# Pooled attention and an MLP mixer in one kernel: the first batch's row maxima as the bias of the exponential, loads of q and k changed about, and a new order of the first steps

## The chip, the cores and the metric

The kernel runs on one core of a Trainium2 chip. The metric is the device time of one execution in microseconds, the median of several runs.

## What is computed

Eight batches, eight heads, 576 rows, 64 columns a head. Keys and values are averaged over groups of 8 rows, so each head has 72 pooled keys. The softmax of q times the pooled keys weighs the pooled values. Then a mixer over tokens (576 to 256 to 576) and one over channels (512 to 1536 to 512), each with a residual.

```python
k_p = k.reshape(B, H, Sp, pool, D).mean(axis=3)      # Sp = 72, pool = 8
v_p = v.reshape(B, H, Sp, pool, D).mean(axis=3)
scores = scale * np.matmul(q, k_p.transpose(0, 1, 3, 2))   # scale = 1/8
scores = scores - np.max(scores, axis=-1, keepdims=True)
attn = np.exp(scores)
attn = attn / (np.sum(attn, axis=-1, keepdims=True) + 1e-09)
x = np.matmul(attn, v_p)                             # heads side by side: B, 576, 512
h = np.maximum(xt @ w_tok1, 0.0) @ w_tok2            # xt = x, tokens last
u = x + h.transpose(0, 2, 1)
out = u + np.maximum(u @ w_ch1, 0.0) @ w_ch2
```

## The kernel before

**Rows.** Of a batch's 576 rows the first 512 are laid out four to a partition (row 4p + j); the last 64, the tail, share a 128-partition tile with another batch's tail. A batch's attention is three units: `a` (j = 0, 1), `c` (j = 2, 3) and the tail `t`. In the code `a, c, t` are batch 0's, `a1, c1, t1` batch 1's, and so on.

**One unit's steps.** `qT` turns q by matrix transposes and `copy_qT` copies it out of PSUM. `S(i)` makes the scores of one PSUM bank: bank 0 holds heads 0 to 2, bank 1 heads 3 to 5, bank 2 heads 6 and 7, each with two rows j and 72 columns (432, 432 and 288 columns). `shift(i)` is VectorE's: a maximum over each 72 columns (line 396) and a subtraction that writes `sh` to SBUF (line 398). `do_E(i)` is ScalarE's Exp of a whole bank with the scale 1/8 (line 406), into `prob_m`. `PT` turns the probabilities on TensorE, `copy_PT` copies them out (line 421 on either engine, line 544 for the tail), `AV` multiplies with the pooled values (lines 443, 445), `norm` divides (lines 451, 452). Pooled keys come from `pool_half` and `copy_half` for batch 0 (lines 308 to 320), from `sum_k` and `copy_k` for batch 1, both by matmuls with `pool_m`; pooled values from `pool_v` and `copy_v` (line 349). `prob_m` and `prob_t` are padded from 72 to 128 columns for the transposes that a DMA does in later batches; `clear_probs` zeroes that padding (all of `prob_t`).

**Token and channel mix.** `A_step` and `A` multiply with w_tok1 (line 635), `act_A` is a relu, `u` multiplies with w_tok2 (line 651, and line 649 for an identity), `turn_u` and `copy_uT` turn the result. The channel mix makes `GT` (lines 1007 and 1039) and then the output tiles in three parts each (line 1023), part 2 with the last third of w_ch2. w_tok2 is loaded as `w2r`, and GpSimd copies it into `w2m` (`split_w_tok2`, line 245), which line 651 reads.

**Order.** All loads with a change of type (fp32 to bf16) are issued by GpSimd in one queue, in the order of the calls at the end of the function (`load`, `load_w_tok`, `load_w_ch1`, ...). Half of batch 0's k comes by SyncE as fp32 and is converted by VectorE (line 210). The compute engines follow an order written out by hand: `begin()` lists the first steps, one call a line, and each engine runs its own in that order. The first list (batch 0's attention and token mix, to `weave(Stream(), st)`) is issued as it stands. The second (batch 1's attention and token mix) is woven into batch 0's channel mix by `weave`, which compares the running sums of the given costs. `fill`, `warm` and the numbers behind `S` and `AV` are idle matmuls on a zero tile (line 261) that keep TensorE busy. PSUM has six buffers `pa` and two `pt`, each given on in the order in which they come free.

Of the kernel before, what the change touches and what calls it, by code (L numbers as in the profile page):

```python
# [48 lines left out]
def kernel(  # L49
# [67 lines left out]
    def load(b, which=(0, 1, 2)):  # L117
        g = group_of[b]
        if (b == 2 or g > 1 and slot_of[b] == 0) and b not in main_t:
            tail_t[b] = [tail_pool.tile([P, H, D], BF16, name=n) for n in ("kt", "qt")]  # L120
            if b == 2:
                for t in tail_t[b]:
                    nc.gpsimd.memset(t[half[0]], 0.0)
            else:
                tail_t[groups[g][1]] = tail_t[b]
        main_t.setdefault(b, [None] * 3)
        for i in which:
            src = (k, q, v)[i]
            if i == 2 and b > 1:

                main_t[b][i] = v_pool.tile([P, H, POOL, D], BF16, name="vs")
                if b != 3:
                    load_v(b)
                continue
            mt = (v_pool.tile([P, H, POOL, D], BF16, name="vs")[:, :, 0:NJ, :] if i == 2 else
                  kv_pool.tile([P, H, NJ, D], BF16, name=("km", "qm")[i]))
            main_t[b][i], tt = mt, tail_t[b][i]
            nc.gpsimd.dma_start(out=mt.rearrange("p h j d -> p h (j d)"),
                                in_=src[b, :, 0:MAIN, :].rearrange("h (p j) d -> p h (j d)", j=NJ))

            for bb in [b] if g < 2 else groups[g] if slot_of[b] == 0 else []:
                nc.gpsimd.dma_start(out=tt[half[slot_of[bb]]], in_=src[bb, :, MAIN:S, :].rearrange("h p d -> p h d"))
# [30 lines left out]
    nc.vector.memset(pool_m, 1.0 / POOL)  # L173
# [7 lines left out]
    nc.vector.memset(diag, 1.0 / POOL)  # L181
# [31 lines left out]
    prob_m = [singles.tile([P, 2, H, P], BF16, name=f"prob_m{i}") for i in range(NPB)]  # L213
    prob_t = [singles.tile([P, 2, HP, P], BF16, name=f"prob_t{i}") for i in range(2)]
# [133 lines left out]
    def copy_v(b):  # L348
        nc.scalar.activation(out=vpx[b % NB][:, :, 0:D], in_=vp_of[b], func=AF.Copy, scale=float(POOL))
# [11 lines left out]
    class Unit:  # L361
# [31 lines left out]
        def shift(self, i):  # L393
            sc, n = self.sc[i], (BANKS[i][1] - BANKS[i][0]) * 2
            mx = sm_pool.tile([P, 8], FP32, name="mx")
            nc.vector.tensor_reduce(out=mx[:, 0:n], in_=sc, axis=AX.X, op=ALU.max)  # L396
            sh = sh_pool.tile([P, 6, SP], FP32, name="sh")
            nc.vector.tensor_tensor(out=sh[:, 0:n], in0=sc, in1=mx[:, 0:n, None].broadcast_to([P, n, SP]),  # L398
                                    op=ALU.subtract)
            self.sh[i] = sh  # L400

        def do_E(self, i):
            h0, h1 = BANKS[i]
            if self.probs is None:
                self.probs = prob_m[(2 * self.b + self.jj) % NPB]
            nc.scalar.activation(out=self.probs[:, :, h0:h1, 0:SP].rearrange("p e h n -> p h e n"),  # L406
                                 in_=self.sh[i][:, 0:(h1 - h0) * 2].rearrange("p (h e) n -> p h e n", e=2),
                                 func=AF.Exp, scale=scale)
# [68 lines left out]
    class TailUnit:  # L477
# [49 lines left out]
        def do_E(self):  # L527
            self.probs = prob_t[self.g % 2]
            for i, sh in enumerate(self.sh):
                nc.scalar.activation(out=self.probs[:, i, :, 0:SP], in_=sh[:, 0:HP], func=AF.Exp, scale=scale)  # L530
# [223 lines left out]
    def begin():  # L754
# [6 lines left out]
        add(0, fill, 17)  # L761
        add(0, fill, 9)
        add(0, c.qT, 0, HP)
        add(0, pool_half, 0)
        add(0, pool_half, 1)
        add(0, c.copy_qT, 0, HP, nc.scalar.copy)
        add(0, copy_half, 0, 1, nc.scalar.copy)
        add(0, copy_half, 0, 0, nc.vector.tensor_copy)
        add(0, a.qT, 0, HP)
        add(0, c.S, 0, 1)  # L770
        add(0, copy_half, 1, 0, nc.vector.tensor_copy)
        add(0, a.copy_qT, 0, HP, nc.scalar.copy)
        add(0, a.S, 0, 1)
        add(0, c.qT, HP, H)
        add(0, a.qT, HP, H)
        add(0, copy_half, 1, 1, nc.scalar.copy)
        add(0, a.copy_qT, HP, H, nc.scalar.copy)
        add(0, a.S, 2)
        add(0, warm, 9)
        add(0, a.S, 1)  # L780
        add(0, a.shift, 0)
        add(0, t.turn_q)
        add(0, c.copy_qT, HP, H, nc.scalar.copy)
        add(0, c.S, 1)
        add(0, a.shift, 2)
        add(0, c.shift, 0)
        add(0, a.do_E, 0)
        add(0, a.shift, 1)
        add(0, c.S, 2)
        add(0, a.do_E, 2)  # L790
        add(0, pool_v, 0)
        add(0, t.copy_qT)
        add(0, a.do_E, 1)
        add(0, c.do_E, 0)
        add(0, a.PT, 0)
        add(0, c.shift, 2)
        add(0, c.shift, 1)
        add(0, c.do_E, 2)
        add(0, a.copy_PT, 0, nc.vector.tensor_copy)
        add(0, t.S)  # L800
        add(0, a.PT, 1)
        add(0, t.shift)
        add(0, copy_v, 0)
        add(0, a.AV, 0, 1)
        add(0, c.do_E, 1)
        add(0, a.copy_PT, 1, nc.scalar.copy)
        add(0, t.do_E)
        add(0, a.norm, 0)
        add(0, c.PT, 0)
        add(0, a.AV, 1, 1)  # L810
        add(0, c.copy_PT, 0, nc.scalar.copy)
# [3 lines left out]
        add(0, t.PT)  # L815
        add(0, c.copy_PT, 1, nc.scalar.copy)
        add(0, c.norm, 0)
        add(0, c.AV, 1)
        add(0, t.copy_PT, nc.scalar.copy)
        add(0, c.norm, 1)  # L820
        add(0, t.AV)
        add(0, t.norm)
        add(0, m0.A_step, (0,))
        add(0, m0.A_step, (1,))
        add(0, m0.A_step, (2,))
        add(0, m0.A_step, (3,))
        add(0, m0.A_step, (4,))
        add(0, m0.act_A, 0)
        add(0, a1.qT)
        add(0, m0.act_A, 1)  # L830
        add(0, m0.u, 2)
        add(1800, a1.copy_qT, 0, H, nc.vector.tensor_copy)
        add(0, m0.u, 1)
        add(0, m0.add_u, 2)
        add(0, m0.u, 0)
        add(0, m0.add_u, 1)
        add(0, m0.add_u, 0)
        add(0, m0.u, 3)
        add(0, m0.turn_u, 1)
        add(0, m0.turn_u, 0)  # L840
        add(0, m0.add_u, 3)
        add(0, sum_k, 1)
        add(0, m0.turn_u, 2)
        add(0, m0.copy_uT, 1, nc.vector.tensor_copy)
        add(1170, copy_k, 1, 1)
        add(0, m0.copy_uT, 0, nc.scalar.copy)
        add(0, m0.copy_uT, 2, nc.vector.tensor_copy)
        add(0, m0.turn_u, 3)
        add(0, copy_k, 1, 0)
        add(0, m0.copy_uT, 3, nc.vector.tensor_copy)  # L850
# [4 lines left out]
        add(0, a1.S, 1)  # L855
        add(0, c1.qT)
        add(0, t1.turn_q)
        add(0, a1.S, 0)
        add(0, a1.S, 2)
        add(1170, c1.copy_qT, 0, H, nc.scalar.copy)  # L860
        add(0, load, 3, (2,))
        add(0, c1.S, 0)
        add(1060, a1.shift, 1)
        add(1060, a1.shift, 0)
        add(0, c1.S, 1)
        add(0, a1.do_E, 1)
        add(0, load_v, 3, 0, 2)
        add(848, a1.shift, 2)
        add(0, a1.do_E, 2)
        add(1800, t1.copy_qT)  # L870
        add(0, a1.do_E, 0)
        add(1378, c1.shift, 0)
        add(1060, c1.shift, 1)
        add(0, pool_v, 1)
        add(0, c1.S, 2)
        add(0, a1.PT, 0)
        add(0, sum_v, 2)
        add(212, c1.shift, 2)
        add(0, c1.do_E, 0)
        add(216, copy_v, 1)  # L880
        add(0, c1.do_E, 1)
        add(0, c1.do_E, 2)
        add(0, a1.PT, 1)
        add(0, t1.S)
        add(1060, t1.shift)
        add(350, a1.copy_PT, 1, nc.scalar.copy)
        add(0, pair_k, 3)
        add(1400, a1.copy_PT, 0, nc.vector.tensor_copy)
        add(1150, a1.do_AV, 0)
        add(0, t1.do_E)  # L890
        add(0, c1.PT, 0)
        add(1400, c1.copy_PT, 0, nc.vector.tensor_copy)
        add(0, c1.PT, 1)
        add(140, c1.copy_PT, 1, nc.scalar.copy)
        add(0, t1.PT)
        add(910, t1.copy_PT, nc.vector.tensor_copy)
        add(1495, c1.do_AV, 0)
        add(0, c2.qT)
        add(1495, t1.do_AV)
        add(1150, c1.do_AV, 1)  # L900
        add(920, a1.do_AV, 1)
        add(0, sum_k, 2)
        add(1170, c2.copy_qT)
        add(0, m1.A, 0)
        add(180, copy_k, 2, 1)
        add(864, m1.act_A, 0)
# [3 lines left out]
        add(0, a2.qT)  # L910
        add(0, m1.u, 2)
        add(0, copy_k, 2, 0)
        add(138, m1.add_u, 1)
        add(0, m1.u, 3)
        add(690, m1.add_u, 3)
        add(0, m1.u, 0)
        add(552, m1.add_u, 2)
        add(720, a2.copy_qT)
        add(0, sum_v, 3, 0, 2)
        add(138, m1.add_u, 0)  # L920
        add(0, m1.uT, 2, 2)
        add(0, m1.uT, 0, 2)
        add(0, t2.turn_q)
        add(900, t2.copy_qT)
# [158 lines left out]
    load(2, (1, 0, 2))  # L1083
# [43 lines left out]
```

## Time and profile before

| | us |
|---|---|
| median of 3 runs | 280.03 (279.56 to 281.25) |
| the profiled execution | 279.91 |
| its span, first to last instruction | 277.8 |
| TensorE busy | 267.6 (96%) |
| VectorE, ScalarE, GpSimd busy | 166.0, 121.8, 113.3 |
| granted TensorE clock | 1.0 throughout |

In the lines of the profile PE is TensorE and PEld its weight loads, DVE VectorE, ACT ScalarE, POOL GpSimd, SP SyncE; a q behind the name is the engine's sequencer. L398 is line 398 of the kernel. In the timeline a row gives the start and the duration in us, the engine, the line, the operation, what it writes and reads, the shape, how many were merged, and in brackets how long the engine was idle before it and who ended that. The view of the loads gives the median time from issue to landing of the loads issued in a stretch.

### The profile page before, as it was taken

How to read it: one execution, taken by the hardware profiler on the slowest of the kernel's cores; microseconds unless marked ns; L12 is line 12 of the kernel's file. 1: busy time of each engine (PE TensorE's matmuls, PEld its weight loads, DVE VectorE, ACT ScalarE, POOL GpSimd, SP SyncE). 2: the span in 40 equal slices, each digit the busy share in tenths (PEclk: the TensorE clock that was granted, in tenths of full speed). 3: DMA queues.
4: the chain of work that ended last, by engine and by line, in shares of the span. 5: the costliest groups of instructions: out<-in, count | busy, mean ns of one | idle time of the engine just before them, and what ended most of it. 6: DMA issues, size and time to landing. Idle time of an engine off the chain costs nothing.

```text
span 277.8 us, 5476 instructions
## 1 busy us (share of the span) xinstructions
PE 267.6 (96%) x2144; PEld 145.2 (52%) x2172; DVE 166.0 (60%) x383; ACT 121.8 (44%) x225; POOL 113.3 (41%) x160
## 2 busy tenths in 40 slices
PE   6789999999999999999999999999999999999994
PEld 4465856554545454474545454475545454554463
DVE  6597677778759852694479762775479452520112
ACT  8673688235533463045534452054623550036220
POOL 8758434696539857185349263930000000000000
PEclk9999999999999999999999999999999999999999
DMA  8999999996999999979997999858376700461013
GB/s 140 185 195 206 199 205 196 190 206 135 200 151 190 213 245 155 227 158 175 166 184 149 191 200 189 177 138 143 82 78 154 186 4 38 113 97 38 38 40 113
DMA packets 98969, 42.27 MB, mean 152 GB/s; under 512 B 68800, under 2 KB 94400, under 8 KB 98944
## 3 DMA queue, kind: packets, MB, share of 16 engines
q0 software_dynamic: 35616, 17.93, 49.6%
q1 hardware_dynamic: 63184, 23.93, 42.1%
q8 instruction: 17, 0.28, 0.4%
q10 hardware_dynamic: 144, 0.07, 0.1%
q14 instruction: 8, 0.07, 0.1%
HBM read 35.85 MB, written 9.44 MB: 163 GB/s over the span
## 4 chain that ended last, share of the span: by engine, by line
PE 89%; DVE 4%; DMA 2%; ACT 1%; issue 1%; POOL 1%; DVEq 0%; POOLq 0%
PE pa L1023 33%; PE pa L1007 31%; PE pa L672 3%; PE pa L390 3%; PE pa L468 3%; DMA km<-in_k_dram 2%; PE pa L597 2%; PE pa L651 1%; PE pa L615 1%; DVE xm L473 1%; PE pt L615 1%; PE pa L1039 1%; PE pt L374 1%; PE pa L677 1%; PE pa L635 1%
## 5 line engine op out<-in xcount | busy, mean ns | idle before, releaser
L1023 PE MATMUL pa<-wc,GT 128*128 128x512 bf16 (+2 forms) x426 | 102.5, 373 | 1.0 <-issue 0.2
L1009 ACT ACTIVATE GT<-pa 128x512 bf16<-128x512 f32 x105 | 62.1, 597 | 61.7 <-PE pa L1007 61.5
L1007 PE MATMUL pa<-uTm,wc 128*128 128x512 bf16 x372 | 89.1, 379 | 0.0
L1007 PEld LDWEIGHTS <-wc 128*128 128x128 bf16 x564 | 45.0, 98 | 36.7 <-issue 1.0
L1023 PEld LDWEIGHTS <-GT 128*128 128x128 bf16 x444 | 40.8, 98 | 41.5 <-issue 1.2
L406 ACT ACTIVATE prob_m<-sh 128x432 bf16<-128x432 f32 (+1 forms) x48 | 24.5, 522 | 55.2 <-DVE sh L398 55.1
L1027 DVE TENSOR_TENSOR o<-pa,um 128x512 f32<-128x512 f32 (+2 forms) x33 | 22.1, 670 | 28.6 <-PE pa L1023 28.5
L357 POOL TENSOR_TENSOR s<-vs 72x512 f32<-72x512 bf16 x24 | 27.6, 1150 | 14.8 <-DMA vs<-in_v_dram 13.4
L398 DVE TENSOR_TENSOR sh<-pa,mx 128x432 f32<-128x432 f32 (+1 forms) x48 | 26.8, 558 | 4.1
L396 DVE TENSOR_REDUCE mx<-pa 128x6 f32<-128x432 f32 (+1 forms) x48 | 26.4, 550 | 4.5 <-PE pa L390 4.3
L473 DVE TENSOR_TENSOR xm<-pa,den 128x256 bf16<-128x256 f32 x56 | 23.7, 424 | 1.9
L472 DVE RECIPROCAL den<-pa 128x4 f32<-128x4 f32 x60 | 10.5, 176 | 17.7 <-PE pa L468 17.5
L1055 POOL DMA_DIRECT2D out_dram<-o x1 | 0.6, 622 | 48.6 <-DVE o L1027 48.6
L673 DVE TENSOR_TENSOR um<-pa,xm 128x512 bf16<-128x512 f32 x24 | 16.1, 688 | 5.6 <-PE pa L672 4.3
L358 POOL TENSOR_TENSOR s<-s 72x256 f32<-72x256 f32 x24 | 17.3, 721 | 1.9
L390 PE MATMUL pa<-kbd,qT 128*128 128x144 bf16 x128 | 15.2, 226 | 0.9 <-ACT qT L378 0.7
L390 PEld LDWEIGHTS <-qT 128*128 128x128 bf16 x128 | 10.6, 98 | 9.3 <-ACT qT L378 1.3
L468 PEld LDWEIGHTS <-pT 72*128 72x128 bf16 (+1 forms) x256 | 11.4, 100 | 7.1 <-issue 0.8
L672 PE MATMUL pa<-AT,w2m 128*128 128x512 bf16 x45 | 13.1, 379 | 0.0
L468 PE MATMUL pa<-vpx,pT 72*128 72x65 bf16 (+1 forms) x256 | 12.6, 194 | 0.0
L269 POOL COPY kk<-km 128x1024 bf16<-128x1024 bf16 x8 | 8.1, 1037 | 10.8 <-DMA km<-in_k_dram 10.8
L1007 PE MATMUL pa<-uTt,wc 128*128 128x128 bf16 x192 | 11.9, 219 | 0.0
(151 smaller groups left out, 269.1 us busy)
## 6 DMA issues: line engine op xcount, KB each, us to landing
out_dram<-o SPq DMA_DIRECT2D x30, 256.0 KB, 2.6
vs<-in_v_dram POOLq DMA_DIRECT2D x7, 512.0 KB, 11.1
km<-in_k_dram POOLq DMA_DIRECT2D x7, 512.0 KB, 9.5
qm<-in_q_dram POOLq DMA_DIRECT2D x7, 512.0 KB, 12.7
wc<-in_moe_w_ch_dram POOLq DMA_DIRECT2D x6, 512.0 KB, 11.8
out_dram<-o SPq DMA_DIRECT2D x8, 128.0 KB, 2.4
o<-in_k_dram SPq DMA_DIRECT2D x2, 256.0 KB, 2.9
kt<-in_k_dram POOLq DMA_DIRECT2D x8, 64.0 KB, 7.8
```

The costliest lines, as they stand in the source:

```text
L357: nc.gpsimd.tensor_tensor(out=s4, in0=vs[:, hs, 0:4], in1=vs[:, hs, 4:8], op=add)
L390: nc.tensor.matmul(out=sc[:, (h - h0) * 2:(h - h0) * 2 + 2, :], lhsT=qTs[self.b][:, 2 * h + self.jj, :], rhs=kbd[self.b % NB][:, h], start ...
L396: nc.vector.tensor_reduce(out=mx[:, 0:n], in_=sc, axis=AX.X, op=ALU.max)
L398: nc.vector.tensor_tensor(out=sh[:, 0:n], in0=sc, in1=mx[:, 0:n, None].broadcast_to([P, n, SP]), op=ALU.subtract)
L406: nc.scalar.activation(out=self.probs[:, :, h0:h1, 0:SP].rearrange("p e h n -> p h e n"), in_=self.sh[i][:, 0:(h1 - h0) * 2].rearrange("p ...
L468: nc.tensor.matmul(out=ao[r, hh, :], lhsT=probs_of(h, r), rhs=vpx[b % NB][:, h, :], start=True, stop=True)
L473: nc.vector.tensor_tensor(out=xo[rows, hf * HP * D:(hf + 1) * HP * D].rearrange("p (h d) -> p h d", d=D), in0=ao[rows, :, 0:D], in1=den[ro ...
L672: nc.tensor.matmul(out=u_ps, lhsT=w2m[:, m, j, :], rhs=ATs[b][:, m, :], start=(m == 0), stop=(m == 1))
L1007: nc.tensor.matmul(out=g_ps[:, i, :], lhsT=wc1[:, kk, m * P:(m + 1) * P], rhs=uTs(kk, 0, width), start=(kk == 0), stop=(kk == 3))
L1009: nc.scalar.activation(out=GT[:, m0:m0 + per, :], in_=g_ps, func=AF.Relu)
L1023: nc.tensor.matmul(out=hold["ps"], lhsT=GT[:, kk, j * P:(j + 1) * P], rhs=wc2[:, kk, cols], start=(kk == 0), stop=(kk == NM - 1))
L1027: nc.vector.tensor_tensor(out=o_sb, in0=hold["ps"], in1=us(j)[:, cols], op=ALU.add)
```

## The change

- **Scale.** The 1/8 of the softmax moves into the pooling matrices (`pool_m`, `diag`), Exp loses its scale, and `copy_v` multiplies by pool/scale. (1/8 is exact in bf16.)
- **Maximum as bias.** `shift(i, True)` makes the negated maximum alone and leaves the scores in PSUM; `do_E` then runs one Exp for each head and row j, 72 columns, with that maximum as its bias. Three banks of batch 0 do so: `c` bank 0, `a` banks 0 and 1. The others stay as they were.
- **Loads.** q's first half goes ahead of k's tail. w_tok goes ahead of batch 1's k and q; the last third of w_ch1 ahead of `split_w_tok2`; the last third of w_ch2 behind batch 2.
- **Clears.** `prob_m` and `prob_t` become one tile, and one GpSimd memset of its padding stands behind the first third of w_ch1. Two memsets for batch 2's tails go from GpSimd to VectorE.
- **Order.** Both lists of `begin()` are rewritten: some copies change between ScalarE and VectorE, idle matmuls are placed anew, one token-mix step stands ahead of the tail's values, and the weave puts batch 1's `m1.A` ahead of the third part of the first output tile.

```diff
+    load_main0(q, main_t[0][1], 0, HP)
     load_tail0(k, tail_t[0][0])
-    load_main0(q, main_t[0][1], 0, HP)
...
-    nc.vector.memset(pool_m, 1.0 / POOL)
+    nc.vector.memset(pool_m, scale / POOL)
...
-    prob_m = [singles.tile([P, 2, H, P], BF16, name=f"prob_m{i}") for i in range(NPB)]
-    prob_t = [singles.tile([P, 2, HP, P], BF16, name=f"prob_t{i}") for i in range(2)]
+    prob_all = singles.tile([P, NPB + 1, 2, H, P], BF16, name="probs")
+    prob_m = [prob_all[:, i] for i in range(NPB)]
+    prob_t = [prob_all[:, NPB, i].rearrange("p (e h) n -> p e h n", e=2) for i in range(2)]
...
-        for t in prob_m:
-            nc.any.memset(t.rearrange("p e h n -> p (e h) n")[:, :, SP:P], 0.0)
-        for t in prob_t:
-            nc.any.memset(t, 0.0)
+        nc.gpsimd.memset(prob_all.rearrange("p t e h n -> p (t e h) n")[:, :, SP:P], 0.0)
...
-        def shift(self, i):
+        def shift(self, i, biased=False):
             sc, n = self.sc[i], (BANKS[i][1] - BANKS[i][0]) * 2
             mx = sm_pool.tile([P, 8], FP32, name="mx")
+            if biased:
+                nc.vector.tensor_reduce(out=mx[:, 0:n], in_=sc, axis=AX.X, op=ALU.max, negate=True)
+                self.sh[i] = (sc, mx)
+                return
...
+            if isinstance(self.sh[i], tuple):
+                sc, low = self.sh[i]
+                for h in range(h0, h1):
+                    for e in range(2):
+                        o = 2 * (h - h0) + e
+                        nc.scalar.activation(out=self.probs[:, e, h, 0:SP], in_=sc[:, o, :], func=AF.Exp,
+                                             bias=low[:, o:o + 1])
+                return
...
+        add(0, fill, 11)
+        add(0, fill, 16)
+        add(0, pool_half, 0)
         add(0, c.qT, 0, HP)
         add(0, pool_half, 1)
+        add(0, a.qT, 0, HP)
+        add(0, c.qT, HP, H)
         add(0, c.copy_qT, 0, HP, nc.scalar.copy)
+        add(0, a.qT, HP, H)
+        add(0, a.copy_qT, 0, HP, nc.vector.tensor_copy)
         add(0, c.S, 0, 1)
+        add(0, a.S, 0)
+        add(0, c.shift, 0, True)
+        add(0, a.shift, 0, True)
...
+        add(0, c.AV, 1, 1)
         add(0, t.copy_PT, nc.scalar.copy)
+        add(0, m0.A_step, (0,))
+        add(0, t.AV)
...
+    load_w_tok()
     load(1, (0, 1))
-    load_w_tok()
     load_w_ch1(0)
+    clear_probs()
     load_w_ch1(1)
     load_w_ch2(0)
     load(1, (2,))
+    load_w_ch1(2)
     split_w_tok2()
-    load_w_ch1(2)
     load_w_ch2(1)
+    load(2, (1, 0, 2))
     load_w_ch2(2)
-    clear_probs()
-    load(2, (1, 0, 2))
     load(3, (1, 0))
```

More of the change, by code (lines that the diff above doesn't have):

```diff
@@ L122, in load @@
                 for t in tail_t[b]:
-                    nc.gpsimd.memset(t[half[0]], 0.0)
+                    nc.vector.memset(t[half[0]], 0.0)
             else:
@@ L348, in copy_v @@
     def copy_v(b):
-        nc.scalar.activation(out=vpx[b % NB][:, :, 0:D], in_=vp_of[b], func=AF.Copy, scale=float(POOL))
+        nc.scalar.activation(out=vpx[b % NB][:, :, 0:D], in_=vp_of[b], func=AF.Copy, scale=POOL / scale)
     def sum_v(b, h1=0, h2=H):
@@ L889, in begin @@
[L889 to L891 removed]
+        add(0, load, 3, (2,))
+        add(848, a1.shift, 0)
+        add(0, a1.S, 1)
+        add(1170, c1.copy_qT, 0, H, nc.vector.tensor_copy)
+        add(0, c1.S, 0)
+        add(0, a1.S, 2)
+        add(530, a1.shift, 1)
+        add(0, a1.do_E, 1)
+        add(212, a1.shift, 2)
+        add(1060, c1.shift, 0)
+        add(0, c1.S, 1)
+        add(1378, c1.shift, 1)
+        add(0, a1.do_E, 0)
+        add(0, c1.S, 2)
@@ new lines, in begin @@
+        add(0, a1.do_E, 2)
+        add(0, pool_v, 1)
+        add(0, a1.PT, 0)
+        add(0, c1.do_E, 0)
+        add(212, c1.shift, 2)
+        add(1800, t1.copy_qT)
+        add(0, c1.do_E, 1)
+        add(0, t1.S)
+        add(910, a1.copy_PT, 0, nc.vector.tensor_copy)
+        add(0, c1.do_E, 2)
+        add(0, load_v, 3, 0, 2)
+        add(0, sum_v, 2)
+        add(1060, t1.shift)
+        add(540, copy_v, 1)
+        add(0, c1.PT, 0)
+        add(0, t1.do_E)
+        add(0, a1.PT, 1)
+        add(560, a1.copy_PT, 1, nc.scalar.copy)
```

161 lines of the change are left out of this document (62 added, 99 removed).

## Prediction

> **What bounds the kernel now.** I read the page first, then the engines' busy time by stretches, then the chain of waits over the first 24 us, then that stretch instruction by instruction.
>
> ```profile
> span 277.8 us, 5476 instructions
> ...
> 30.20:64.00 33.80, 33.64 (x319) 20.35 (x320) 25.84 (x61) 19.03 (x36) 19.24 (x26) 1.00 1.33 190
> 64.00:274.30 210.30, 208.77 (x1504) 108.00 (x1524) 118.89 (x270) 82.74 (x151) 72.02 (x96) 1.00 0.82 143
> ```
>
> The second and third rows give a stretch, its length, and TensorE's busy time in it. From 30.2 us to the last matmul TensorE idles 0.16 + 1.53 us. That work is not changed, only some of it is put in another order, so after 30 us there is nothing to gain and only new waits can cost. The time follows from when this dense work begins. The chain before it:
>
> ```profile
> 14.82 0.62 DVE mx L396
> ...
> 17.61 0.61 DVE sh L398
> ...
> 19.77 0.44 ACT prob_t L530
> 20.21 1.88 ACT pT L421 x2
> 22.14 0.18 PE pa L443
> 23.96 1.67 PE pa L635 x7
> ```
>
> VectorE sets the pace from 14.8 to 19.7 (a maximum and a subtraction for each bank of scores), then ScalarE (the tail's Exp, three copies of turned probabilities), then TensorE (the last values, the token mix of line 635). The first matmul that needs the token mix's result and the split weights w2m is the yardstick for all that follows:
>
> ```profile
> 25.48 0.61 PE L374 MATMUL pt<-ident,qm 128*128 128x128 bf16 x8
> 26.11 0.69 PE L651 MATMUL pa<-AT,w2m 128*128 128x512 bf16 x2
> 22.04 0.58 ACT L544 COPY pT<-pt 72x512 bf16<-72x512 bf16 x1
> 22.68 0.19 PE L443 MATMUL pa<-vpx,pT 72*64 72x1 bf16 x1
> ```
>
> It stands at 26.11, behind ScalarE's last copy (ends 22.62) and the tail's values (22.68). From there the work is full, so what line 651 gains or loses goes into the time one for one.
>
> **The change, part by part.**
>
> *VectorE* loses three subtractions of a 432-wide bank, 0.61 each (line 398 above), 1.8 in all, and hands two halves of q and k copies to and fro with ScalarE. It stops being the bound: from the first scores at 11.7 (below) three maxima, a copy, two banks of 288 and one of 432 with their subtractions add up to some 5.3 with a short wait, so its last subtraction of a bank, now 18.2, comes out near 17. What is late next is ScalarE.
>
> *ScalarE* gets 18 Exps of 72 elements with a bias from memory in place of three of 432 elements. The trace has no such instruction. Its nearest rows:
>
> ```profile
> L406 ACT ACTIVATE prob_m<-sh 128x432 bf16<-128x432 f32 x4 | 2.2, 562 | 1.0 <-DVE sh L398 1.0
> L406 ACT ACTIVATE prob_m<-sh 128x288 bf16<-128x288 f32 x2 | 0.9, 442 | 0.4 <-DVE sh L398 0.4
> ...
> 16.10 1.37 ACT L406 ACTIVATE prob_m<-sh 128x432 bf16<-128x432 f32 x3 [0.69 <-DVE sh L398]
> ...
> 8.89 0.30 DVE L319 CAST kbd<-pa 64x144 bf16<-64x144 f32 x1 [2.38 <-PE pa L312]
> 9.09 0.28 ACT L319 CAST kbd<-pa 64x144 bf16<-64x144 f32 x1
> 9.38 0.27 ACT L320 CAST kbd<-pa 64x144 bf16<-64x144 f32 x1
> 15.04 0.37 ACT L499 COPY qTt<-pt 128x256 bf16<-128x256 bf16 x1 [0.92 <-PE pt L494]
> ```
>
> 144 elements more cost 0.120, 0.83 ns an element, so 72 elements would take 0.442 - 216 x 0.00083 = 0.26. Three Exps of 0.56 + 0.56 + 0.44 ran in 1.37, so neighbours overlap by 0.1: **0.16** from one to the next is the lower bound. The two casts, which read PSUM like the new Exps, follow each other by 0.29 without overlap; the shortest ScalarE instruction that reads PSUM over all 128 partitions takes 0.37, which is the **upper** bound. I take 0.23, between the Exp rows and the casts, nearer the Exps since the form is theirs. So its new work is 18 x 0.23 = 4.14, where three wide Exps took 3 x 0.46.
>
> Here a rule speaks against the change. The Trainium skill, page ScalarE: Activation LUTs, section What ACT_TABLE_LOAD costs, says that a bias given as a pointer to a column adds about 93 ns to each ACTIVATE, and that neighbours overlap by as much. By its formula a 72-element Exp takes 0.34 and follows the last by 0.25, 18 of them 4.45, and the path below would end 0.3 later than I make it. No row of before has a bias pointer; the wide Exps fit its formula without one (0.546 against 0.562).
>
> *Where that path starts.* c's scores now stand behind the second half of q, because the transposes of that half are put ahead of them on TensorE; a's scores and all that follows there wait with them:
>
> ```profile
> 3.85 0.76 POOL L153 DMA_DIRECT2D qm<-in_q_dram  x1
> ...
> qm<-in_q_dram POOLq DMA_DIRECT2D x1, 256.0 KB, 6.8
> ...
> 1.34 0.85 POOL L157 DMA_DIRECT2D kt<-in_k_dram  x1 [0.81 <-POOLq L1111]
> ...
> kt<-in_k_dram POOLq DMA_DIRECT2D x1, 64.0 KB, 5.3
> ```
>
> That half lands at 3.85 + 6.8 = 10.65. Then the transposes (0.44 until the next matmul may follow: the 0.61 of line 374 less a matmul's trail of 0.17), one idle matmul and three score matmuls (0.53), and VectorE's maximum (0.61): the first Exp starts at 10.7 + 0.44 + 0.53 + 0.03 + 0.61 = 12.3. With q's first half issued ahead of k's tail, the 64 KB of small pieces no longer fill the quiet start alone. The four loads of k and q carry the same bytes, so the second half of q lands no later than 10.65; were the first to land 5.3 after its issue as k's tail did, up to 0.9 earlier. I take 0.2, near the lower end, since the same bytes have to move.
>
> *ScalarE from there*, each step at its row's duration less 0.1 overlap: 18 new Exps 4.14; two Exps of 288 and one of 432, 0.34 + 0.34 + 0.46; the tail's q 0.27; v, a copy of probabilities, the tail's Exp, two copies, the last copy:
>
> ```profile
> 17.37 0.58 ACT L349 ACTIVATE vpx<-pa 72x512 bf16<-72x512 f32 x1
> 18.72 0.99 ACT L421 COPY pT<-pt 72x1024 bf16<-72x1024 bf16 x1
> ```
>
> 0.48 + 0.99 + 0.35 + 1.9 + 0.58. In all 12.3 + 4.14 + 5.7 = 22.15, against 22.62. One token-mix step (two of line 635's matmuls, 0.43 by its 1.67 for seven) is moved ahead of the tail's values, into the wait for ScalarE's last copy. c's last values start at 22.15 - 0.58 + 0.05 = 21.6 and take 0.54 (22.14 to 22.68), the step 0.43: the tail's values at 22.6. Before it was 22.68 and 3.43 on to line 651, now 3.0: **25.6, or 25.4** with the 0.2 from the loads.
>
> *GpSimd* gets the clear of the probabilities' spare columns, 5 x 2 x 8 rows of 56 = 4480 elements a partition, in the middle of its queue. Behind it stand five loads and then the split that writes w2m (line 245). What it issues:
>
> ```profile
> 13.57 0.54 POOL L239 DMA_DIRECT2D w1t<-in_moe_w_tok_dram  x1 [1.95 <-DMA vs<-in_v_dram]
> ...
> 8.77 0.72 POOL L142 DMA_DIRECT2D kt<-in_k_dram  x1
> 9.45 0.93 POOL L138 DMA_DIRECT2D qm<-in_q_dram  x1
> 10.32 0.74 POOL L142 DMA_DIRECT2D qt<-in_q_dram  x1
> 17.35 1.55 POOL L250 DMA_DIRECT2D wc<-in_moe_w_ch_dram  x2 [1.99 <-DMA km<-in_k_dram]
> 21.01 0.90 POOL L138 DMA_DIRECT2D vs<-in_v_dram  x1
> 21.93 0.69 POOL L142 DMA_DIRECT2D vt<-in_v_dram  x1
> 23.35 1.22 POOL L245 COPY w2m<-w2r 128x512 bf16<-128x512 bf16 x2 [0.73 <-DMA w2r<-in_moe_w_tok_dram]
> 3.71 0.23 POOL masks.py:197 MEMSET ident<- 128x128 bf16 x1
> 26.72 0.56 POOL L123 MEMSET kt<- 64x512 bf16 x1
> ```
>
> 384 elements more cost 0.33, 0.86 ns each: the clear takes 4.0. Bounds: 2.0 if it wrote two at a time, 5.1 at the 1.14 ns of line 245's copies. The first row shows that a load waits for the landing of the one eight before it, v's at 13.3. In the new order k's tail of batch 1 is that load, at 13.57; after it GpSimd has no wait, since each load's partner has landed: 0.68 + 0.87 + 0.68 (starts of the rows above), four of wc 3.1, clear 4.0, v 0.92 + 0.69, split 1.2: w2m is ready at 13.57 + 12.1 = **25.7, or 25.5** with the 0.2. Before, it waited for the transfer of w2r instead and ended at 24.57. This is the later of the two paths, though by little: line 651 starts near 25.55 in place of 26.11, a gain of 0.55.
>
> *Hidden parts.* The clears leave ScalarE and VectorE early, where both wait anyway (VectorE 2.38 ahead of 8.89); so do batch 2's two tail memsets, two short ones for VectorE. One idle matmul more ahead of 8 us, two fewer later, lie in waits. w_tok goes ahead of batch 1's k and q; its last big load is now the one that the split waits for until 23.35, and the bytes of both together are the same, so batch 1's q lands about then, and its first use is at 25.48 (cover 2; without it line 651 waits as long).
>
> *The channel weights* behind batch 2's loads:
>
> ```profile
> 38.16 0.59 POOL L146 DMA_DIRECT2D vs<-in_v_dram  x1 [2.62 <-DMA wc<-in_moe_w_ch_dram]
> ...
> vs<-in_v_dram POOLq DMA_DIRECT2D x1, 64.0 KB, 12.9
> ...
> 50.33 1.04 PE L1023 MATMUL pa<-wc,GT 128*128 128x512 bf16 x3
> ```
>
> The last third of w_ch2 now lands where batch 2's v did, 38.16 + 12.9 = 51.1. It is needed by the third part of the first output tile, now 50.33. But the new order puts batch 1's token mix (2.2) and 0.7 of transposes ahead of that part: 52.8 after the gain. Cover 1.7.
>
> The order after line 651 is new in many small places; I charge 0.15 for it. **Sum:** -0.55 + 0.15 = -0.4 on the profiled execution's 279.91 (2.1 of it outside its span), which lies 0.12 under the median of 280.03: **279.5 us**.
>
> **Rivals.**
>
> *ScalarE becomes the bound* (slower). Place: its unbroken run from 12.3 to 22; price: 18 times what an Exp costs over 0.23. From 0.26 on it is slower than before (25.4 + 18 x 0.03 = 25.95, with the 0.15 no gain is left). At 0.33, between the cast's 0.29 and the 0.37, line 651 starts at 27.2: 281.2. For it: ScalarE has no idle time there, and the casts do not overlap. Against: neighbouring Exps do.
>
> *Cheap Exps and a short clear.* 0.16 and 2.0: line 651 at 25.4 - 1.26 = 24.15, 278.1; with VectorE's normalisations in between I say 278.4. For it: the Exp rows. Against: memset rows at 0.86 ns.
>
> *The clear holds the split.* At 5.1, w2m at 26.6: +0.5 + 0.15, 280.6. The rows for copies speak for it, those of memsets against.
>
> *The clear holds the Exps*, if the probabilities, now one tile, were ordered behind it as a whole: the first Exp waits for 13.57 + 2.2 + 0.8 + 4.0 = 20.6, 8.3 late, so 288. Against it: at 8.89 and 9.09 VectorE and ScalarE wrote interleaved columns of one tile at the same time.
>
> **How the numbers follow.** Forecast 0.50 (own range 278.9 to 280.2), ScalarE the bound 0.20, cheap 0.15, split held 0.10, Exps held 0.05. Range 278.3 (the cheap case) to 282.0 (an Exp at 0.37: 25.4 + 2.5 = 27.9, +1.8 + 0.15, and a little for new waits). One per cent, 2.8 us, is about what a measurement of this kernel tells from no change: faster by that needs all lower bounds and more, 0.02; slower, the held Exps and half the upper tail, 0.09; within, 0.89.
>
> **What would show it.** Right: the new Exps 0.2 to 0.26 apart; ScalarE without idle time from about 12.3 to 22; a GpSimd memset near 4 us between the loads of wc; line 651 between 25.2 and 25.9 with GpSimd's split or ScalarE's relu as releaser; no TensorE wait over 0.3 from there to 64 us. Wrong: VectorE still the releaser of the copies, an Exp that waits for GpSimd, TensorE waiting for w_ch2 near 52 us, or line 651 after 26.3.

## Result and the profile after

| | before | changed |
|---|---|---|
| median, us (range) | 279.93 (279.55 to 281.25) | 279.31 (278.62 to 280.89) |
| the profiled execution | 279.91 | 279.35 |
| its span | 277.8 | 277.3 |

The changed kernel takes 0.9979 of the time before, 95% interval 0.997 to 0.9989: 0.6 us faster, inside the one per cent called no change. 279.5 was predicted.

First the stretches from the start of the dense work, the counterpart of the two rows shown of before (start:end, length, TensorE's busy time and matmuls, then the other engines):

```profile
span 277.3 us, 5510 instructions
29.85:64.00 34.15, 34.15 (x324) 20.70 (x322) 26.04 (x61) 19.46 (x37) 19.83 (x27) 1.00 1.34 191
64.00:273.90 209.90, 209.69 (x1524) 107.58 (x1521) 118.45 (x270) 82.61 (x150) 71.76 (x96) 1.00 0.81 143
```

The dense work begins 0.35 earlier (29.85 against 30.20) and is as long as it was: 34.15 + 209.90 = 244.05 against 33.80 + 210.30 = 244.10. So the gain was made ahead of it.

The chain that ended last, over the first 26 us (start, duration, what):

```profile
3.84 6.65 DMA qm<-in_q_dram
10.54 0.64 PE pt L372 x8
11.20 0.44 DVE qT L376
11.65 0.31 DVE kbd L317
11.98 0.31 DVE kbd L318
12.32 0.62 DVE mx L395
12.96 2.64 ACT probs L413 x12
...
25.76 0.38 PE pa L661
```

Where VectorE stood with a maximum and a subtraction for each bank, q's landing, three short VectorE copies with one maximum, and ScalarE's new Exps (line 413) stand now. Line 661 is the yardstick, line 651 of before: 25.76 against 26.11, which is the 0.35. (The two profiled executions differ by 0.56 in time. 0.40 of it is there at the end of the second stretch, 273.90 against 274.30; the other 0.16 lies behind it, 0.10 in the rest of the span and 0.06 outside the span.)

The timeline of ScalarE, VectorE, GpSimd and TensorE, one behind the other (brackets: idle time before the instruction, and who ended it):

```profile
12.96 2.64 ACT L413 ACTIVATE probs<-pa,mx 128x72 bf16<-128x72 f32 x12 [0.34 <-DVE mx L395]
15.41 0.53 ACT L416 ACTIVATE probs<-sh 128x288 bf16<-128x288 f32 x1
...
18.03 0.64 ACT L416 ACTIVATE probs<-sh 128x432 bf16<-128x432 f32 x1
...
19.81 1.92 ACT L431 COPY pT<-pt 72x1024 bf16<-72x1024 bf16 x2
21.75 0.58 ACT L554 COPY pT<-pt 72x512 bf16<-72x512 bf16 x1
25.11 0.60 ACT L601 ACTIVATE AT<-pa 128x512 bf16<-128x512 f32 x1 [2.79 <-PE pa L645]
...
16.72 0.61 DVE L400 TENSOR_TENSOR sh<-pa,mx 128x432 f32<-128x432 f32 x1
...
16.41 3.88 POOL L223 MEMSET probs<- 128x4480 bf16 x1
...
23.95 1.29 POOL L243 COPY w2m<-w2r 128x512 bf16<-128x512 bf16 x2
...
11.61 0.55 PE L388 MATMUL pa<-kbd,qT 128*128 128x144 bf16 x6 [0.27 <-ACT qT L376]
...
21.79 0.18 PE L453 MATMUL pa<-vpx,pT 72*128 72x1 bf16 x1
...
22.77 0.19 PE L453 MATMUL pa<-vpx,pT 72*64 72x1 bf16 x1
...
25.76 0.69 PE L661 MATMUL pa<-AT,w2m 128*128 128x512 bf16 x2
```

Between the Exps at 12.96 and the end of the last copy at 22.33 no bracket stands: ScalarE is never idle. Twelve Exps fill 12.96 to 15.41, 0.204 each. GpSimd's split is done at 25.24, ScalarE's relu (line 601) at 25.71, and TensorE's own matmuls ahead of line 661 at 25.74; line 661 starts at 25.76, so these legs end close to each other. The profile's chain leaves ScalarE at 17.27 and follows TensorE, which has no gap from 17.32 on, idle matmuls among its work. ScalarE has hardly more to spare: the second of its two copies at 19.81 ends at 21.73, and the values that read it start at 21.79.

### The profile page after: what moved, and what is told of

It is laid out like the page before. It is cut to its first block, busy times and chain, and to the rows that moved or that the text cites. A ratio compares the mean times of both kernels' runs of the same rounds, so it can differ in the third digit from the quotient of the medians.

```text
span 277.3 us, 5510 instructions
## 1 busy us (share of the span) xinstructions
PE 269.7 (97%) x2174; PEld 145.2 (52%) x2174; DVE 164.0 (59%) x379; ACT 121.6 (44%) x237; POOL 116.2 (42%) x159
## 4 chain that ended last, share of the span: by engine, by line
PE 90%; DVE 3%; DMA 2%; ACT 2%; POOL 1%; issue 1%; POOLq 0%
PE pa L1033 34%; PE pa L1017 31%; PE pa L682 4%; PE pa L478 3%; PE pa L388 3%; DMA qm<-in_q_dram 2%; PE pa L607 2%; PE pt L428 1%; ACT probs L413 1%; PE pa L661 1%; PE pa L625 1%; PE pt L625 1%; DVE xm L483 1%; PE pa L1049 1%; PE pt L372 1%; PE pa L645 1%
## 5 line engine op out<-in xcount | busy, mean ns | idle before, releaser
L1033 PE MATMUL pa<-wc,GT 128*128 128x512 bf16 (+2 forms) x444 | 104.1, 374 | 0.0
L416 ACT ACTIVATE probs<-sh 128x432 bf16<-128x432 f32 (+1 forms) x45 | 22.9, 524 | 56.8 <-DVE sh L400 56.8
L400 DVE TENSOR_TENSOR sh<-pa,mx 128x432 f32<-128x432 f32 (+1 forms) x45 | 24.9, 554 | 3.8
L398 DVE TENSOR_REDUCE mx<-pa 128x6 f32<-128x432 f32 (+1 forms) x45 | 24.6, 546 | 3.2 <-PE pa L388 3.0
L478 PEld LDWEIGHTS <-pT 72*128 72x128 bf16 (+1 forms) x256 | 11.5, 99 | 6.8 <-issue 0.8
L682 PE MATMUL pa<-AT,w2m 128*128 128x512 bf16 x48 | 13.8, 379 | 0.0
L259 PE MATMUL pa<-idle 128*128 128x288 bf16 (+2 forms) x42 | 10.2, 389 | 2.2 <-DVE idle L168 2.2
L603 DVE TENSOR_SCALAR AT<-pa 128x512 bf16<-128x512 f32 x6 | 4.2, 692 | 13.1 <-PE pa L611 7.3
```

Of the source, the lines that this page charges most:

```text
L478: nc.tensor.matmul(out=ao[r, hh, :], lhsT=probs_of(h, r), rhs=vpx[b % NB][:, h, :], start=True, stop=True)
L682: nc.tensor.matmul(out=u_ps, lhsT=w2m[:, m, j, :], rhs=ATs[b][:, m, :], start=(m == 0), stop=(m == 1))
L1033: nc.tensor.matmul(out=hold["ps"], lhsT=GT[:, kk, j * P:(j + 1) * P], rhs=wc2[:, kk, cols], start=(kk == 0), stop=(kk == NM - 1))
```

## Experiments

Line 651 or 661, whichever the kernel has, is called the token mix's second product below.

**1. The bias taken out of the changed kernel.**

```diff
-        add(0, c.shift, 0, True)
+        add(0, c.shift, 0, False)
...
-        add(0, a.shift, 0, True)
+        add(0, a.shift, 0, False)
...
-        add(0, a.shift, 1, True)
+        add(0, a.shift, 1, False)
```

> The changed kernel with its new order, loads and clear, but the three banks keep the subtraction on VectorE and the one wide Exp. Theory (the bias takes VectorE off the path): VectorE's last bank subtraction, 17.33 in the changed kernel, ends 3 x 0.61 later, near 19.1; the Exp behind it starts at 19.2 in place of 18.03 and ScalarE's last copy and line 661 come 1.1 later, near 26.8; time about 280.4, a little slower than before. Rival (the new order and loads bring the gain, the bias is idle): line 661 stays at 25.8, time 279.3.

Measured: 280.65 us, ratio to before 1.0022 (1.001 to 1.0035). From its timeline:

```profile
18.21 0.61 DVE L400 TENSOR_TENSOR sh<-pa,mx 128x432 f32<-128x432 f32 x1
18.86 0.56 ACT L416 ACTIVATE probs<-sh 128x432 bf16<-128x432 f32 x1 [0.17 <-DVE sh L400]
...
26.72 0.69 PE L661 MATMUL pa<-AT,w2m 128*128 128x512 bf16 x2
```

VectorE is the releaser again, its last subtraction ends at 18.82, and the second product comes at 26.72: the new order, loads and clear without the bias are slower than before. The bias is worth some 1.3 us in that order (280.65 less 279.31).

**2. The bias alone, in the kernel before.** `shift`, `do_E` and the scale as in the change; in the old list of steps:

```diff
-        add(0, a.shift, 0)
+        add(0, a.shift, 0, True)
...
-        add(0, c.shift, 0)
+        add(0, c.shift, 0, True)
...
-        add(0, a.shift, 1)
+        add(0, a.shift, 1, True)
```

> The kernel before, old order, loads and clears, with the maximum as bias for the same three banks. Theory: the old order lets the first Exp start at 12.7, as early as the changed kernel's 12.96; ScalarE then works without idle time: 18 Exps at 0.205, two of 288, one of 432, v and the tail's q make 18.3 less what starts earlier, so the last bank's Exp starts near 17.85 in place of 18.25 and the last copy ends near 22.2; its line 651 comes near 25.7 (before 26.11), time 279.5: the bias alone gives the whole gain. Rival (order and loads bring it): 26.1 and 279.9.

Measured: 280.48 us, 1.002 (1.0011 to 1.0028). Neither theory expected that the bias alone would be slower. Its ScalarE and the second product:

```profile
14.96 0.37 ACT L511 COPY qTt<-pt 128x256 bf16<-128x256 bf16 x1 [0.64 <-PE pt L506]
15.39 2.65 ACT L415 ACTIVATE prob_m<-pa,mx 128x72 bf16<-128x72 f32 x12
...
18.65 0.61 ACT L418 ACTIVATE prob_m<-sh 128x432 bf16<-128x432 f32 x1
...
26.40 0.69 PE L663 MATMUL pa<-AT,w2m 128*128 128x512 bf16 x2
```

The copy of the tail's turned q stands in ScalarE's order ahead of twelve Exps, and ScalarE idles 0.64 for it. Before, there was time for that: the engine waited for VectorE anyway (0.92 idle ahead of the same copy). Now that ScalarE carries the path, the wait counts: the last bank's Exp starts at 18.65, before at 18.25. The load is not what holds the copy in this trace: the tail's q landed at 14.15 (7.25 + 6.9), while TensorE's transposes of it start at 14.64, in its order behind nine idle matmuls (from 12.41) and three of the scores.

**3. The same with one call moved,** c's six Exps ahead of that copy:

```diff
         add(0, a.do_E, 2)
+        add(0, c.do_E, 0)
         add(0, pool_v, 0)
         add(0, t.copy_qT)
         add(0, a.do_E, 1)
-        add(0, c.do_E, 0)
```

> The kernel before with the bias alone (old order, loads, clears), with one call moved: c's bank 0 Exps ahead of the tail's copy of q on ScalarE. There the bias alone was slower than before because ScalarE idled 0.76 ahead of and behind that copy, whose source lands at 14.2, with six Exps ready. Theory (ScalarE's unbroken run sets line 651, and the order has to keep it unbroken): the last bank's Exp starts near 17.7 in place of 18.65, line 651 near 25.5 to 25.7 in place of 26.40, time 279.4 to 279.7, faster than before: the bias gains once the order fits. Rival (the old order holds elsewhere, on TensorE's turned probabilities or VectorE): 26.2 or later, 280.2 or more.

Measured: 279.43 us, 0.9985 (0.9976 to 0.9994).

```profile
15.31 0.47 ACT L511 COPY qTt<-pt 128x256 bf16<-128x256 bf16 x1
...
17.60 0.66 ACT L418 ACTIVATE prob_m<-sh 128x432 bf16<-128x432 f32 x1
...
25.39 0.69 PE L663 MATMUL pa<-AT,w2m 128*128 128x512 bf16 x2
```

The idle time is gone, the last bank's Exp starts 1.05 earlier, and the second product follows by 1.01. One moved line turns the bias from a loss of 0.5 us into a gain of 0.3 to 0.4, with the old loads and clears. What the new order must do is keep ScalarE's run unbroken. This is about as far as the whole change got: 0.9985 and 0.9979 have intervals that overlap, so what the new loads, the clear and the rest of the new order add to the bias is not shown.

**4. The clear behind the last load.**

```diff
     load_w_ch1(0)
-    clear_probs()
...
     load(3, (1, 0))
+    clear_probs()
```

> The changed kernel with the clear of the probabilities' padding moved behind the last load of the list. GpSimd's split of w_tok2, which ends at 25.25 in the changed kernel, is then done near 21.4. Theory (ScalarE and TensorE set line 661, the split has 0.5 to spare): line 661 stays at 25.76, time 279.3 within 0.1. Rival (GpSimd's queue sets it): line 661 about 0.5 earlier, 278.8.

Measured: 279.03 us, 0.9974 (0.9959 to 0.9989).

```profile
22.42 1.23 POOL L243 COPY w2m<-w2r 128x512 bf16<-128x512 bf16 x2
...
25.71 0.69 PE L661 MATMUL pa<-AT,w2m 128*128 128x512 bf16 x2
```

The split ends 1.6 earlier (23.65) and the second product starts where it did. In these profiled executions GpSimd does not set it. The time is lower by 0.28, within what the intervals leave open.

**5. One wide Exp a bank in place of six.** The first head's maximum serves all six; the kernel leaves the others out.

```diff
-                for h in range(h0, h1):
-                    for e in range(2):
-                        o = 2 * (h - h0) + e
-                        nc.scalar.activation(out=self.probs[:, e, h, 0:SP], in_=sc[:, o, :], func=AF.Exp,
-                                             bias=low[:, o:o + 1])
+                nc.scalar.activation(out=self.probs[:, :, h0:h1, 0:SP].rearrange("p e h n -> p h e n"),
+                                     in_=sc.rearrange("p (h e) n -> p h e n", e=2), func=AF.Exp, bias=low[:, 0:1])
```

> The changed kernel with one Exp of 432 elements a bank in place of six of 72, straight from PSUM, with the first head's maximum as the bias of all six (the other heads' own maxima are left out). ScalarE saves 18 x 0.205 - 3 x 0.46 = 2.3. Theory: it then waits for VectorE's last subtraction, 17.33, so the last bank's Exp starts 0.6 earlier than 18.03 and line 661 could come at 25.2, but GpSimd's split (25.25) holds it near 25.3: time 278.8. Rival (ScalarE's Exps count one for one): 24 to 24.5, time 277.5. Rival (GpSimd sets it already): 25.76, time 279.3.

Measured: 278.74 us, 0.996 (0.9947 to 0.9974).

```profile
12.32 1.13 ACT L410 ACTIVATE probs<-pa,mx 128x432 bf16<-128x432 f32 x2 [0.34 <-DVE mx L395]
...
24.74 0.39 PE L658 MATMUL pa<-AT,w2m 128*128 128x512 bf16 x1
25.32 0.39 PE L658 MATMUL pa<-AT,w2m 128*128 128x512 bf16 x1 [0.19 <-POOL w2m L243]
```

The first Exp starts 0.64 earlier here (q had landed earlier), so 0.38 of the 1.02 by which the second product is ahead is the cheaper Exps' work, where 2.3 of ScalarE's time was taken away. Now GpSimd's split is the releaser. That is the second leg, close behind the first.

**6. The 18 Exps without a bias.** 

```diff
-                        nc.scalar.activation(out=self.probs[:, e, h, 0:SP], in_=sc[:, o, :], func=AF.Exp,
-                                             bias=low[:, o:o + 1])
+                        nc.scalar.activation(out=self.probs[:, e, h, 0:SP], in_=sc[:, o, :], func=AF.Exp)
```

> The changed kernel with its 18 Exps of 72 elements, but without a bias (the maximum is left out). In the changed kernel they follow each other by 0.205. Theory A (the price of an Exp this small is its own fixed part and its elements, the pointer to the bias costs nothing extra): they still follow each other by 0.20. Theory B (the pointer costs extra time in each): they follow by 0.16, the lower bound taken from the wide Exps. By either the first starts up to 0.6 earlier, since no maximum is waited for, and GpSimd's split (25.25) holds line 661 near 24.8 to 25.3.

Measured, one execution: 279.81 us. The timeline's row, then the first twelve Exps (duration in ns: least, median, most), without a bias and with it (the changed kernel):

```profile
12.87 1.59 ACT L413 ACTIVATE probs<-pa 128x72 bf16<-128x72 f32 x12 [0.34 <-DVE mx L395]
...
L413 ACT ACTIVATE probs<-pa x12: 225/281/350, 12.9 to 14.1; 128x72 bf16<-128x72 f32 x12
```

```profile
L413 ACT ACTIVATE probs<-pa,mx x12: 313/350/396, 13.0 to 15.2; 128x72 bf16<-128x72 f32 x12
```

They follow each other by (1.59 - 0.35) / 11 = 0.113 without the bias and by (2.64 - 0.396) / 11 = 0.204 with it: 0.091 for the pointer, 1.6 us for all 18. Both theories missed: A had no price for the pointer, and B took the 0.16 that the prediction had drawn from wide Exps as a floor. The Exps did not start earlier: the row still names VectorE's maximum (line 395) as what ended ScalarE's wait, though they no longer read it, and why is open. The run's total says little: v and the tail's q landed late in it, GpSimd's split came late too, and the second product stood at 25.98.

**7. Scores of bank 0 ahead of q's second half.** The chain above says that the start of ScalarE's run waits for q's second half (landing 10.49), though bank 0 needs the first half only.

```diff
-        add(0, c.qT, HP, H)
         add(0, c.copy_qT, 0, HP, nc.scalar.copy)
-        add(0, a.qT, HP, H)
         add(0, a.copy_qT, 0, HP, nc.vector.tensor_copy)
         add(0, c.S, 0, 1)
-        add(0, copy_half, 1, 1, nc.vector.tensor_copy)
         add(0, a.S, 0)
+        add(0, c.qT, HP, H)
+        add(0, a.qT, HP, H)
+        add(0, copy_half, 1, 1, nc.vector.tensor_copy)
```

> The changed kernel, but ScalarE's and VectorE's copies of q's first half and the scores of bank 0 of c and a stand ahead of the transposes of q's second half, so that the first maxima no longer wait for that half's landing (10.5). Theory (ScalarE's unbroken run sets line 661, and its start is bought late by that wait): the first biased Exp starts near 11.8 in place of 12.96 (ScalarE still has a's second copy of q ahead of it), everything behind moves by about 1.1 until GpSimd's split, first part done near 24.6, holds line 661 near 24.7; time 278.3. Rival (the wait for q is covered by a later one, as v or VectorE): 25.7 and 279.3.

Measured: 279.38 us, 0.9983 (0.9969 to 0.9997): no gain over the changed kernel. The first Exp did start at 11.9, but:

```profile
16.82 0.77 POOL L248 DMA_DIRECT2D wc<-in_moe_w_ch_dram  x1 [1.13 <-DMA w1m<-in_moe_w_tok_dram]
17.57 3.85 POOL L223 MEMSET probs<- 128x4480 bf16 x1
...
25.87 0.39 PE L661 MATMUL pa<-AT,w2m 128*128 128x512 bf16 x1 [1.00 <-POOL w2m L243]
```

TensorE waits a full 1.00 for the split. In this execution a load ahead of the clear waited 1.13 for an earlier one to land, which in the changed kernel's profile it did not. The clear and the split came that much later. What ScalarE gained, GpSimd gave back. The twelve runs spread from 278.53 to 280.29, and only this one has a trace, so the wait need not be the same in all of them.

**8. Both: early scores, and the clear behind the last load** (the diffs of 7 and 4 together).

> Scores of bank 0 ahead of q's second half, and the clear behind the last load. Theory: the first Exp near 11.8, and with the split done by 23.7 nothing of GpSimd's holds line 661, which comes 1.1 earlier than 25.76, at 24.6: 278.2, the same as without the moved clear or 0.1 less. Rival (the split is what held): much faster than with the early scores alone.

Measured: 278.58 us (278.16 to 278.70), 0.9955 (0.9942 to 0.9968), the lowest so far with every part of the computation kept. It lies below the changed kernel's 0.9979, whose interval (0.997 to 0.9989) just clears this one.

```profile
12.07 2.65 ACT L413 ACTIVATE probs<-pa,mx 128x72 bf16<-128x72 f32 x12
...
24.88 0.69 PE L661 MATMUL pa<-AT,w2m 128*128 128x512 bf16 x2
```

The first Exp is 0.89 earlier, the second product 0.88. The rival's sentence came true as well: with the early scores the split is what held.

**9. Two biased banks in place of three,** on top of that.

```diff
-        add(0, a.shift, 1, True)
+        add(0, a.shift, 1, False)
```

> As the last, with two banks biased (bank 0 of c and of a) and a's bank 1 with the subtraction. ScalarE loses 6 x 0.205 - 0.46 = 0.77, VectorE gains 0.61, where it has 0.7 to spare before the last bank's Exp. Theory: ScalarE's run ends 0.3 to 0.6 earlier, line 661 near 24.2, time 277.8. Rival (VectorE is back as the bound): line 661 as with three banks or later, 278.3 or more.

Measured: 278.49 us, 0.9952 (0.9938 to 0.9967): the same as with three. ScalarE lost 0.77 of work, but from its first Exp to the last bank's it took 5.07 as against 5.06 with three, since it waited for VectorE instead.

**10. VectorE's first maximum ahead of its copy of k, ScalarE's second copy of q to VectorE, four idle matmuls for seven, a's bank 2 ahead of its bank 1,** also on top of 8.

```diff
-        add(0, copy_half, 1, 1, nc.vector.tensor_copy)
         add(0, c.shift, 0, True)
...
         add(0, a.shift, 0, True)
+        add(0, c.do_E, 0)
+        add(0, copy_half, 1, 1, nc.vector.tensor_copy)
+        add(0, a.copy_qT, HP, H, nc.vector.tensor_copy)
         add(0, c.copy_qT, HP, H, nc.vector.tensor_copy)
-        add(0, a.copy_qT, HP, H, nc.scalar.copy)
-        add(0, a.S, 1, 1)
+        add(0, warm, 4)
         add(0, a.S, 2, 1)
-        add(0, c.do_E, 0)
-        add(0, warm, 7)
-        add(0, a.shift, 1, True)
+        add(0, a.S, 1, 1)
         add(0, t.turn_q)
         add(0, c.S, 2)
         add(0, a.shift, 2, False)
+        add(0, a.shift, 1, True)
```

> As the kernel with early scores and late clear, with VectorE's first maximum ahead of its copy of k and ScalarE's last copy of q given to VectorE; a's bank 2 ahead of its bank 1, four idle matmuls for seven. Theory (ScalarE's unbroken run sets line 661): the first Exp starts near 11.4 in place of 12.07, ScalarE loses a copy of 0.5, VectorE's last subtraction stays near 17, so the last bank's Exp starts at 17.0 to 17.1 in place of 17.13 and line 661 comes 0 to 0.2 earlier than 24.88: 278.3 to 278.6. Rival (TensorE or the tail's q, landing near 14.2, sets the pace there): no gain or a new idle time on ScalarE ahead of the tail's copy, 278.6 to 279.

Measured: 278.45 us (278.03 to 280.81), 0.9961 (0.9946 to 0.9976): no further gain shown. The profiled execution, 280.81, was the longest of them, so its trace shows why this one was late and not what holds the others:

```profile
15.10 0.29 PE L504 MATMUL pt<-ident,qt 64*128 64x64 bf16 x4 [1.90 <-DMA qt<-in_q_dram]
```

The tail's q had landed late, and TensorE and ScalarE stood for it.

**11. The loads in the old order,** with the clear in the queue, **and 12. the same with the clear behind the last load.**

```diff
-    load_main0(q, main_t[0][1], 0, HP)
     load_tail0(k, tail_t[0][0])
+    load_main0(q, main_t[0][1], 0, HP)
...
-    load_w_tok()
     load(1, (0, 1))
+    load_w_tok()
...
-    load_w_ch1(2)
     split_w_tok2()
+    load_w_ch1(2)
     load_w_ch2(1)
-    load(2, (1, 0, 2))
     load_w_ch2(2)
+    load(2, (1, 0, 2))
```

> The changed kernel with the loads in the old order (k's tail ahead of q, w_tok behind batch 1's k and q, the last third of w_ch2 ahead of batch 2), the bias, the clear and the new order of steps kept. Theory (the order of the loads is worth 0.15 at the start and nothing later): the first Exp starts near 13.1, the clear now lies in GpSimd's wait for k near 18, the split ends near 26 and holds line 661 near 25.9 to 26.2; time 279.5 to 279.8. Rival (the loads bring half of the gain or more): 26.5 and 280.

> The changed kernel with the loads in the old order, and the clear behind the last load. With the old loads and the clear in the queue, line 661 came at 26.37, held by GpSimd's split. Theory (the old loads hurt only because they push the clear, and with it the split, back): the split ends near 24.6 to 25 as in the kernel before, ScalarE's run sets line 661 at 25.8 to 25.9, 0.1 later than in the changed kernel since q's second half lands 0.15 later; time 279.3 to 279.5. Rival (the old loads cost time by themselves, later on): line 661 at 25.9 but 279.9 or more.

Measured: 280.42 us, 1.0023 (1.0008 to 1.0038), with the clear in the queue; 279.77, 0.9992 (0.9982 to 1.0001), with the clear at the end. The first, then the second kernel:

```profile
18.04 0.79 POOL L248 DMA_DIRECT2D wc<-in_moe_w_ch_dram  x1 [2.68 <-DMA km<-in_k_dram]
18.82 3.85 POOL L223 MEMSET probs<- 128x4480 bf16 x1
...
26.37 0.39 PE L661 MATMUL pa<-AT,w2m 128*128 128x512 bf16 x1 [0.50 <-POOL w2m L243]
```

```profile
w1m<-in_moe_w_tok_dram POOLq DMA_DIRECT2D x1, 256.0 KB, 11.5
...
22.48 0.60 PE L645 MATMUL pa<-xm,w1m 128*128 128x512 bf16 x2
...
26.01 0.69 PE L661 MATMUL pa<-AT,w2m 128*128 128x512 bf16 x2
```

With the old loads GpSimd stands 2.68 for k ahead of the clear, and the split holds TensorE by 0.50. With the clear gone from there the split ends at 25.36 and no longer holds, but the token mix's first step, which the new order puts ahead of the tail's values, starts as w_tok1 lands (issued at 10.98, 11.5 later: 22.48), where in the changed kernel it starts at 22.24. So the old loads cost in two ways in these profiles, and the theory had only the first. The totals show the first alone: 0.9992 with the clear at the end and the changed kernel's 0.9979 have intervals that overlap. Loads, order and clear can't be priced one by one. With the clear in the queue the time came 0.6 above the upper end that the theory had given, and at the end of the list 0.3 (there the kernel before, run beside it, took 280.09).

## Why the prediction was right, step by step

The total was right to 0.2 us, and the mechanism (VectorE off the path, then ScalarE and GpSimd close to each other) held. Three sizes in it were off, and partly made up for each other.

- **VectorE.** Its last bank subtraction was to end near 17 and ended at 17.33; the timeline has it at 16.72 for 0.61. It releases no copy any more. Shown by experiment 1.
- **An Exp's price: mis-sized.** 0.23 was taken, 0.204 measured. All 18 took 3.68 (12 in 2.45, 6 in 1.23, each from the first start to the start of the next instruction) in place of 4.14: 0.46 less. The step that failed is the floor of 0.16: it was drawn from Exps of 288 and 432 elements, and the same small Exp without a bias ran at 0.113. That 0.204 lies between the ends was luck of two errors, a fixed part too high and no term for the pointer. The rule of the Trainium skill, page ScalarE: Activation LUTs, section What ACT_TABLE_LOAD costs, had that term: about 93 ns for a bias given as a pointer, and experiment 6 measured 91. Its total was too dear here: by its formula, an estimate, an Exp takes 0.34 and follows by 0.25, and the shortest took 0.313 and followed by 0.204, so neighbours overlap by 0.11, not by 0.093.
- **Where ScalarE's run starts: mis-sized.** 12.3 was predicted, 12.96 came. q landed 0.16 earlier than before (10.49 against 10.65), where 0.2 was foreseen. From the landing to the first Exp the prediction summed 1.65, and 2.47 came: the sum had transposes, scores and a maximum, but left out what two engines do in between by their order: TensorE waits 0.27 for the copies of the turned q, and VectorE, the chain shows, makes a copy of q and two of k (11.20 to 12.29) ahead of its maximum. That is 0.82 more, or 0.66 after q's 0.16, of which the cheaper Exps gave 0.46 back.
- **ScalarE unbroken to the last copy.** This held. Predicted end 22.15, measured 22.33 without idle time. From the last copy on, 22.6 and 3.0 to the second product were predicted for the tail's values, and 22.77 and 2.99 measured: 25.76 against 25.4 to 25.6.
- **GpSimd.** The clear was to take 4.0 and took 3.88, the split to end at 25.5 or 25.7 and ended at 25.24. The prediction made this the later leg by 0.1; in the profile it is the earlier by 0.47. Experiments 5, 7 and 11 show it as the holder as soon as ScalarE is quicker or a load late, so "the clear holds the split" is a rival that decides in some kernels and not in this profiled execution.
- **The new order.** 0.15 was charged, and nothing came: the dense stretch is 0.05 shorter, and from 25.76 to 64 us TensorE is busy for the whole 38.24. That charge was a guess. The 1.53 us of TensorE's idle time that the prediction read after 64 us should not have been read so: the row of before holds 1504 matmuls, that of after 1524 for the same work and 0.21 of idle time, in a stretch only 0.4 shorter, so a good part of it is probably matmuls missing from the record (the weight loads in the two rows are nearly the same, 1524 and 1521).
- **One for one.** The prediction let all that the second product gains go into the time. In the fourteen profiled executions that product starts between 24.74 and 27.27, and the time less its start lies between 253.5 and 254.0. So the rule holds to half a microsecond, which is as much as the gain forecast by it.
- **The hidden parts.** w_ch2's last third and its user:

```profile
37.85 0.80 POOL L253 DMA_DIRECT2D wc<-in_moe_w_ch_dram  x1 [2.13 <-DMA wc<-in_moe_w_ch_dram]
...
wc<-in_moe_w_ch_dram POOLq DMA_DIRECT2D x1, 512.0 KB, 13.2
...
52.83 0.38 PE L1033 MATMUL pa<-wc,GT 128*128 128x512 bf16 x1
```

It lands at 37.85 + 13.2 = 51.05 (predicted 51.1) and is used at 52.83 (predicted 52.8). The cover held. For the order of the loads the prediction had only 0.2 at the start and covers; experiments 11 and 12 show that it also keeps the clear, the split and w_tok1 off the path, which the prediction did not see.

- **Rivals.** "ScalarE becomes the bound" was half right: ScalarE sets the pace now, but at a price under the 0.26 from which it would have lost. In experiment 2 the same rival came true in another way: not through dearer Exps but through 0.64 of idle time in a run that had become the path. "The clear holds the Exps" fell: they start at 12.96, the clear at 16.41. "Cheap Exps and a short clear" fell too: 0.204 in place of 0.16, and 3.88 in place of 2.0.

## What to carry to other kernels

When work is moved from one engine to another to shorten a path, walk the receiving engine's order for waits that cost nothing until then: here one copy whose source came late turned the change from a gain into a loss, and moving one call in front of it turned it back. Count the second-latest leg too, with the spread of what it hangs on: 0.47 of cover on a queue of loads was gone in the execution of experiment 7, and early scores paid only once the clear had left that queue. And price a small instruction from a small one; a line through two wide ones gave a floor that the chip went under.

## What the runs showed of the hardware that was not expected

- A bias from memory costs ScalarE 0.091 us an Exp of 72 elements (0.204 against 0.113 from one to the next).
- In an unbroken train of these Exps the shown duration grows (0.313 to 0.396) while the spacing stays, so the mean of such a group (0.379 in the groups' view of the changed kernel) is no price; the spacing is.

```profile
L413 ACT ACTIVATE probs<-pa,mx 128x72 bf16<-128x72 f32 x18 | 4.1, 379 | 0.3 <-DVE mx L395 0.3
```

- The same load differs from execution to execution, in kernels that are alike up to its issue: q's second half, issued at about 3.85 each time, took 6.0 us (wide Exps), 6.7 (changed kernel) and 7.2 (two banks) to land, and whatever starts with it moves along. The view of the loads, of the kernel with wide Exps and of the one with two banks:

```profile
qm<-in_q_dram POOLq DMA_DIRECT2D x1, 256.0 KB, 6.0
```

```profile
qm<-in_q_dram POOLq DMA_DIRECT2D x1, 256.0 KB, 7.2
```
